# Sinkhorn routing of a fused attention and mixture-of-experts kernel: sums as addition trees and scalings on POOL, reciprocals on DVE

## The chip, the cores and the metric

The kernel runs on one core of one Trainium2 chip. The metric is the device time of one execution in microseconds (us). The engines named below are PE (matrix multiplier), ACT, DVE and POOL (elementwise engines), and SP, whose queue issues nearly all DMA transfers. Each engine takes its own instructions strictly in the order in which the program put them; an instruction whose operand is not ready holds up everything behind it on that engine.

## What is computed

The reference has two parts. The first is chunked attention (4 x 8 heads, 768 positions, head size 64), which produces `x` with N = 3072 tokens of D = 512. The second, which holds most of the work, is a mixture of E = 8 experts whose weights per token come from a Sinkhorn normalisation:

```python
logits = x @ w_gate                      # 3072 x 8
P = np.exp(logits - logits.max())
for _ in range(8):
    P /= P.sum(1, keepdims=True) + 1e-09     # over the 8 experts of a token
    P /= P.sum(0, keepdims=True) + 1e-09     # over the 3072 tokens
    P *= N / E
for e in range(E):
    h = np.maximum(x @ w1[e], 0.0)           # 512 -> 1024
    out += P[:, e:e + 1] * (h @ w2[e])       # 1024 -> 512
```

## The kernel before

The tokens are cut into 6 units of 512. The program works through 48 pairs of expert and unit: all six units for expert 0, then all six for expert 1, and so on. While expert 0 runs, the attention for later units is mixed in between. A product is made in fp16 with each operand split into a high and a low part, by a Strassen-like scheme of seven block products; on PE a block product is six matmuls of 256 columns (line 1593, targets `px`, `py`, `pz` for the hidden layer and `yx`, `yy`, `yz` for the output). Expert 0's output uses plain matmuls of 512 columns instead (line 2121, target `yp`).

The other engines serve PE: DVE and ACT take finished sums out of PSUM (`c<-px`, line 1662, with `q` as the part that ACT read earlier), apply the relu and split the result into high and low parts (`h<-c,h`, line 1720). For the next expert, `cut` (line 601) forms four sums of weight blocks in a buffer `ws` on POOL, and `split` (lines 513 and 521) turns the raw weights `w1f`, `w2f` and the sums `ws` into fp16 pairs `w`, first on ACT, then on DVE. There is one `ws` buffer, so that the next four POOL sums wait until DVE has split the last ones. The same `split` makes the inputs `x<-xt` and `x<-xs`.

The order on every engine is written at build time by a planner (`Plan.run`): each task has an engine, a cost in us, dependencies and a priority (a smaller number goes first), and the planner simulates the engines with these costs and emits instructions in the order in which it starts the tasks. At run time only that order and the semaphores remain.

The routing is one chain of tasks inside this plan. It starts when the logits of all 3072 tokens stand in the tile `lg` (128 partitions x 24 token tiles x 8 experts) and ends with `pscale`, by which expert 0's stored outputs are scaled when expert 1's output first adds to them. One of its eight rounds is: row sums, reciprocal, scaling and column sums per partition (`rows`, all on DVE), a matmul with a matrix of ones that adds the column sums over the 128 partitions (`cp`, line 1529, on PE), and reciprocal and scaling (`columns`, on DVE). PE's instruction stream holds the eight `cp` products between block products of expert 0.

Of the kernel before, what the change touches and what calls it, by code (L numbers as in the profile page):

```python
# [12 lines left out]
F32 = mybir.dt.float32  # L13
I32 = mybir.dt.int32
AF = mybir.ActivationFunctionType
ALU = mybir.AluOpType
AX = mybir.AxisListType
# [73 lines left out]
class Plan:  # L91
# [14 lines left out]
    def add(self, eng, cost, fn, deps=(), prio=0.0, bufs=(), takes=None, frees=None, dma=0.0, many=False):  # L106
        t = Task()
        t.eng, t.cost, t.fn, t.prio, t.takes, t.frees = eng, cost, fn, prio, takes, frees
        t.ready, t.end, t.then, t.n, t.dma = 0.0, None, [], len(self.tasks), dma
        t.many = many  # L110
        if dma:
            t.cost = cost * ISSUE
        before = {id(d): d for d in deps if d is not None}
        for b in bufs:
            assert not b.closed
            before.update({id(d): d for d in b.before})
            b.users.append(t)
        t.left = len(before)
        for d in before.values():
            d.then.append(t)  # L120
        if frees is not None:
            frees.left += 1
        self.tasks.append(t)
        return t
# [109 lines left out]
def tile_chunked_attn_sinkhorn_moe(  # L234
# [27 lines left out]
    nc = tc.nc  # L262
    P = 128
    B, H, S, D = q.shape
    NM = mem_k.shape[2]
    N, DM = out.shape
    E, _, F = w1.shape
# [15 lines left out]
    NT = N // P  # L283
# [7 lines left out]

    misc = ctx.enter_context(tc.tile_pool(name="misc", bufs=1))
    small = ctx.enter_context(tc.tile_pool(name="small", bufs=1))
    xpool = ctx.enter_context(tc.tile_pool(name="xpool", bufs=1))
    wl1 = ctx.enter_context(tc.tile_pool(name="wl1", bufs=1))
    wl2 = ctx.enter_context(tc.tile_pool(name="wl2", bufs=1))
# [13 lines left out]
    late = {}  # L310
# [5 lines left out]
    one = misc.tile([P, 1], F32, name="one")  # L316
    nc.vector.memset(one, 1.0)
    ones = one.broadcast_to([P, P])
# [4 lines left out]
    lg = misc.tile([P, NT, E], F32, name="lg")  # L323
# [15 lines left out]
    add = plan.add  # L339
# [14 lines left out]
    def begin(n):  # L354

        m = min(n, NU - 1)
        return START + m * TURN + (n - m) * UNIT
# [57 lines left out]
    def bank(group, shape, name):  # L415
        return Bank(group, lambda b: banks(b).tile(shape, F32, tag=f"b{b}", name=name))
# [5 lines left out]
    opened = [None]  # L422
# [65 lines left out]
    def turned_max(m, a, t, pool, prio, name):  # L488

        row = bank(pool, [1, P], f"row_{name}")  # L490
        t = add(
            "PE",
            0.35,
            lambda: nc.tensor.transpose(row.t, m, ident),
            [t],
            prio - FIRM,
            takes=row,
        )
        return add(
            "DVE",  # L500
            0.3,
            lambda: nc.vector.tensor_reduce(a, row.t, axis=AX.X, op=ALU.max),
            [t],
            prio,
            frees=row,
        )
# [486 lines left out]
    tr = {}  # L993
# [438 lines left out]
    def attention():  # L1432
# [22 lines left out]
                yield  # L1455
        values(*pend.pop(0))

    def routing(deps):

        box = {}  # L1460

        m, a = most_of[:, 0, -1:], most_of[0:1, 1, -1:]
        urgent = begin(LATE) + 58.5
        t = add(
            "DVE",
            0.35,
            lambda: nc.vector.tensor_reduce(m, lg, axis=AX.XY, op=ALU.max),
            deps,
            urgent,
        )  # L1470
        t = turned_max(m, a, t, "main", urgent, "lg")
        spread = bank("main", [P, 1], "sp_lg")
        t = add(
            "PE",
            0.2,
            lambda: nc.tensor.matmul(spread.t, ones[0:1], a, start=True, stop=True),
            [t],
            urgent - FIRM,
            takes=spread,
        )  # L1480
        t = add("DVE", 0.15, lambda: nc.vector.tensor_copy(m, spread.t), [t], urgent, frees=spread)
        t = add(
            "DVE",
            0.35,
            lambda: nc.vector.tensor_scalar(lg, lg, m, None, op0=ALU.subtract),
            [t],
            urgent,
        )
        t = add("ACT", 0.35, lambda: nc.scalar.activation(lg, lg, AF.Exp), [t], urgent)

        def rows(it):
            def go():
                rs = small.tile([P, NT], F32, tag="rs", bufs=1, name=f"rs_{it}")
                nc.vector.tensor_reduce(rs, lg, axis=AX.X, op=ALU.add)
                nc.vector.tensor_scalar_add(rs, rs, 1e-9)
                nc.vector.reciprocal(rs, rs)
                nc.vector.tensor_tensor(
                    lg, lg, rs[:, :, None].broadcast_to([P, NT, E]), op=ALU.mult
                )
                box[it] = small.tile([P, E], F32, tag="cs", bufs=1, name=f"cs_{it}")  # L1500
                nc.vector.tensor_reduce(
                    box[it], lg.rearrange("p t e -> p e t"), axis=AX.X, op=ALU.add
                )

            return go

        def columns(it, cp):
            def go():
                cr = small.tile([P, E], F32, tag="cr", bufs=1, name=f"cr_{it}")
                nc.vector.tensor_scalar_add(cr, cp.t, 1e-9)  # L1510
                nc.vector.reciprocal(cr, cr)
                nc.vector.scalar_tensor_tensor(
                    lg,
                    lg,
                    float(N) / float(E),
                    cr[:, None, :].broadcast_to([P, NT, E]),
                    op0=ALU.mult,
                    op1=ALU.mult,
                )

            return go

        for it in range(8):
            t = add("DVE", 1.8, rows(it), [t], urgent)
            cp = bank("main", [P, E], f"cp_{it}")
            t = add(
                "PE",
                0.4,
                lambda it=it, cp=cp: nc.tensor.matmul(
                    cp.t, ones, box[it], start=True, stop=True  # L1530
                ),
                [t],
                urgent,
                takes=cp,
            )
            t = add("DVE", 0.8, columns(it, cp), [t], urgent, frees=cp)

        def finish():
            for u in range(NU):
                us = slice(u * TU, (u + 1) * TU)  # L1540
                nc.vector.tensor_scalar(
                    lg[:, us], lg[:, us], ux[:, u : u + 1], 2.0**HSHIFT, op0=ALU.mult, op1=ALU.mult
                )

        return add("DVE", 1.4, finish, [t], urgent)
# [642 lines left out]
    for n, (e, u) in enumerate(units):  # L2188
# [23 lines left out]
        if n == LATE:  # L2212
            while len(lgs) < NU:
                next(feed, None)

            def turn():
                plan.fill = None
                astack.close()
                late["w1"] = ctx.enter_context(tc.tile_pool(name="wr1", bufs=1, side="right"))
                late["w2"] = ctx.enter_context(tc.tile_pool(name="wr2", bufs=1, side="right"))  # L2220
                late["h"] = ctx.enter_context(tc.tile_pool(name="hr", bufs=1, side="right"))
                late["c"] = ctx.enter_context(tc.tile_pool(name="cr", bufs=1, side="right"))
                late["ss"] = ctx.enter_context(tc.tile_pool(name="sr", bufs=1, side="right"))
                for group in ("att", "two"):
                    for b in plan.free[group]:
                        heappush(plan.free["main"], b)
                    plan.free[group] = []

            att_tasks = lgs + [xkept[v] for v in range(KEEP)] + list(gkept.values())
            opened[0] = add("-", 0.0, turn, att_tasks, -2000.0)  # L2230
            for kind, slot in (("w1", 4), ("w2", 4), ("w2", 5), ("h", 4), ("h", 5), ("c", 2), ("ss", 2)):
                rings[kind].after(slot, [opened[0]])
            for kind in ("c", "ss"):
                ring_ = rings[kind]
                ring_.order = [ring_.n % 2, (ring_.n + 1) % 2, 2]
                ring_.n = 0
            for kind, m in (("w1", 5), ("w2", 6), ("h", 6)):
                rings[kind].order = list(range(m))
            rings["w1"].n, rings["w2"].n, rings["h"].n = 4, 4, 4
            routed[0] = routing(lgs)  # L2240
            expert_scale(0, begin(n))
# [81 lines left out]
```

## Time and profile before

| what | value |
|---|---|
| median of 3 runs (lowest to highest) | 1913.08 us (1911.89 to 1914.97) |
| the profiled execution: time / span | 1913.3 us / 1911.5 us |
| granted PE clock | 0.999 |
| PE busy (share of the span) | 1898.8 us (99%) |
| DVE busy | 1468.1 us (77%) |
| ACT busy | 1022.5 us (53%) |
| POOL busy | 503.0 us (26%) |
| first and last of the eight row sums start | 299.8 us, 330.8 us |

The span runs from the first to the last recorded instruction; the time has 1.8 us around it. A busy PE is no proof of PE at its full pace, since a matmul's recorded duration covers its way through the array while the next is already running: the distance between starts shows the pace. Groups of instructions give a count, the total busy time, the mean of one, and after the bar the idle time of the engine before them with what ended it.

### The profile page before, as it was taken

How to read it: one execution, taken by the hardware profiler on the slowest of the kernel's cores; microseconds unless marked ns; L12 is line 12 of the kernel's file. 1: busy time of each engine (PE TensorE's matmuls, PEld its weight loads, DVE VectorE, ACT ScalarE, POOL GpSimd, SP SyncE). 2: the span in 40 equal slices, each digit the busy share in tenths (PEclk: the TensorE clock that was granted, in tenths of full speed). 3: DMA queues.
4: the chain of work that ended last, by engine and by line, in shares of the span. 5: the costliest groups of instructions: out<-in, count | busy, mean ns of one | idle time of the engine just before them, and what ended most of it. 6: DMA issues, size and time to landing. Idle time of an engine off the chain costs nothing.

```text
span 1911.5 us, 47024 instructions
## 1 busy us (share of the span) xinstructions
PE 1898.8 (99%) x19535; PEld 1634.8 (86%) x19535; DVE 1468.1 (77%) x2456; ACT 1022.5 (53%) x1999; POOL 503.0 (26%) x541
## 2 busy tenths in 40 slices
PE   8999999999999999999999999999999999999999
PEld 7777676788888888888888888888888888888888
DVE  5887679878589867898668875898678885786565
ACT  4665555556465545546446544655555563564453
POOL 1210012514134211522224231342124232332112
PEclk9999999999999999999999999999999999999999
DMA  8787653543324432264224433245313632222321
GB/s 198 189 219 182 160 173 133 169 169 106 126 80 160 150 134 77 90 217 165 84 91 154 165 119 114 84 155 188 127 45 111 247 112 97 98 84 83 127 84 67
DMA packets 212998, 254.81 MB, mean 133 GB/s; under 512 B 112240, under 2 KB 146480, under 8 KB 208432
## 3 DMA queue, kind: packets, MB, share of 16 engines
q1 hardware_dynamic: 210660, 251.21, 40.4%
q8 instruction: 153, 2.51, 0.6%
q10 hardware_dynamic: 2124, 0.59, 0.2%
q14 instruction: 61, 0.50, 0.1%
HBM read 187.84 MB, written 63.44 MB: 131 GB/s over the span
## 4 chain that ended last, share of the span: by engine, by line
PE 97%; DVE 2%; SPq 0%; ACT 0%; issue 0%; DMA 0%; POOL 0%; DVEq 0%; POOLq 0%
PE px L1593 26%; PE yx L1593 23%; PE pz L1593 13%; PE yz L1593 11%; PE py L1593 6%; PE yp L2121 6%; PE yy L1593 6%; PE pp L2040 1%; PE xp L1138 1%; PE sp L1071 1%; PE warm L427 1%; DVE w L521 1%; PE ta L1128 1%; PE tk L1012 1%; PE tq L1008 1%; SPq L923 0%
## 5 line engine op out<-in xcount | busy, mean ns | idle before, releaser
L1593 PEld LDWEIGHTS <-w 128*128 128x128 f16 x7896 | 771.2, 98 | 94.4 <-issue 2.8
L1593 PEld LDWEIGHTS <-h 128*128 128x128 f16 x7056 | 690.4, 98 | 81.1 <-issue 0.9
L1593 PE MATMUL px<-x,w 128*128 128x256 f16 x4512 | 547.8, 273 | 1.5 <-DVE c L1662 1.0
L1926 POOL TENSOR_TENSOR acc<-acc,y 128x256 f32<-128x256 f32 x252 | 262.4, 1049 | 881.1 <-ACT y L1901 868.5
L1593 PE MATMUL yx<-w,h 128*128 128x256 f16 x4032 | 467.9, 273 | 0.5 <-DVE acc L1936 0.5
L1652 ACT ACTIVATE q<-px 128x256 f32<-128x256 f32 x376 | 143.1, 382 | 289.6 <-PE px L1593 285.1
L1593 PE MATMUL pz<-x,w 128*128 128x256 f16 x2256 | 278.1, 273 | 0.0
L1593 PE MATMUL yz<-w,h 128*128 128x256 f16 x2016 | 233.8, 273 | 0.0
L1821 DVE TENSOR_TENSOR h<-ss,h 128x1024 f16<-128x1024 f32 x168 | 217.6, 1298 | 3.3 <-ACT h L1797 3.3
L1772 ACT ACTIVATE h<-c 128x768 f16<-128x768 f32 x168 | 140.7, 838 | 112.2 <-DVE c L1662 112.2
L1797 ACT CAST h<-ss 128x1024 f16<-128x1024 f32 x168 | 174.2, 1040 | 39.5 <-DVE ss L1761 39.5
L1761 DVE SCALAR_TENSOR_TENSOR ss<-c,ss 128x256 f32<-128x256 f32 x336 | 176.6, 525 | 8.6
L1805 DVE SCALAR_TENSOR_TENSOR h<-c,h 128x768 f16<-128x768 f32 x168 | 168.7, 1007 | 9.2 <-ACT h L1772 9.1
L1662 DVE SCALAR_TENSOR_TENSOR c<-px,q 128x256 f32<-128x256 f32 x188 | 77.8, 421 | 94.8 <-PE px L1593 85.6
L1901 ACT ACTIVATE y<-yx,pscale 128x256 f32<-128x256 f32 x168 | 79.6, 474 | 120.5 <-PE yx L1593 116.5
L1593 PE MATMUL py<-x,w 128*128 128x256 f16 x1128 | 139.0, 273 | 0.0
L2121 PE MATMUL yp<-w,h 128*128 128x512 f16 x576 | 132.0, 379 | 0.9 <-DVE h L2082 0.9
L1761 DVE SCALAR_TENSOR_TENSOR ss<-c,h 128x512 f32<-128x512 f32 x168 | 125.6, 748 | 1.9 <-ACT h L1749 1.9
L1662 DVE SCALAR_TENSOR_TENSOR c<-py,q 128x256 f32<-128x256 f32 x188 | 78.5, 421 | 62.0 <-PE py L1593 58.7
L1593 PE MATMUL yy<-w,h 128*128 128x256 f16 x1008 | 116.9, 273 | 0.0
L2121 PEld LDWEIGHTS <-h 128*128 128x128 f16 x576 | 55.3, 99 | 60.0 <-DVE h L2082 1.4
L513 ACT ACTIVATE w<-ws,sw 128x1024 f16<-128x1024 f32 (+1 forms) x64 | 69.5, 1090 | 65.7 <-POOL ws L601 65.6
(155 smaller groups left out, 1739.6 us busy)
## 6 DMA issues: line engine op xcount, KB each, us to landing
x<-xkeep SPq DMA_DIRECT2D x28, 1792.0 KB
akeep<-acc SPq DMA_DIRECT2D x168, 256.0 KB
acc<-akeep SPq DMA_DIRECT2D x168, 256.0 KB
w1f<-in_moe_w_dram SPq DMA_DIRECT2D x36, 512.0 KB
w2f<-in_moe_w_dram SPq DMA_DIRECT2D x32, 512.0 KB
w1fm<-in_moe_w_dram SPq DMA_DIRECT2D x28, 512.0 KB
w2fm<-in_moe_w_dram SPq DMA_DIRECT2D x28, 512.0 KB
xkeep<-x SPq DMA_DIRECT2D x6, 1792.0 KB
```

The source lines that it names most:

```text
L513: lambda: nc.scalar.activation(dst(0), src(), AF.Copy, scale=s),
L1593: nc.tensor.matmul(dst.t, a, b, start=(not more and n == 0), stop=(n == end), skip_group_check=more,)
L1652: lambda: nc.scalar.activation(t.t, src.t, AF.Copy, scale=DOWN),
L1662: lambda: nc.vector.scalar_tensor_tensor(c.t[:, o], src.t, DOWN, q.t, op0=ALU.mult, op1=ALU.add),
L1761: lambda: nc.vector.scalar_tensor_tensor(dst(), src(), 0.0, other(), op0=ALU.max, op1=op),
L1772: lambda: nc.scalar.activation(h.t[:, 0, 0:3], c.t, AF.Relu),
L1797: lambda: nc.scalar.copy(h.t[:, 0, 3:7], ss.t),
L1805: lambda: nc.vector.scalar_tensor_tensor(h.t[:, 1, 0:3].rearrange("p a n -> p (a n)"), c.t.rearrange("p a n -> p (a n)"), 0.0, h.t[:, 0, 0 ...
L1821: lambda: spare.tensor_tensor(h.t[:, 1, 3:7], ss.t, h.t[:, 0, 3:7], op=ALU.subtract),
L1901: (lambda: nc.scalar.activation(t.t, src.t, AF.Copy, scale=f))
L1926: lambda: nc.gpsimd.tensor_tensor(acc.t[:, cols], acc.t[:, cols], q.t, op=ALU.add),
L2121: nc.tensor.matmul(py.t, hf.t[:, hl, where[fh], o : o + P], room(fp, WIDE * wl + DM * fh, WIDE * wl + DM * (fh + 1)), start=(fp == 0 and i ...
```

## The change

In each of the eight rounds the row sums become three POOL additions (96, 48 and 24 columns), the row scaling one POOL multiplication of 192 columns, the column sums five POOL additions (96, 48, 24, 8 and 8 columns), and the column scaling one POOL multiplication of 192 columns. DVE keeps the two reciprocals with the additions of 1e-9, and one more instruction on 8 columns that multiplies by N/E. The matmul with ones reads its column sums from the new tile `tree`. The partial results live in `tree`, `row_parts` and `column_parts`. The planner's costs and priorities of these tasks change too: DVE's and PE's parts now go 300 ahead of the rest.

```diff
+        def row_sums():
+            two = tree[0][:, 0 : NT * E // 2].rearrange("p (t e) -> p t e", t=NT)
+            one = tree[0][:, NT * E // 2 :].rearrange("p (t e) -> p t e", t=NT)
+            plus(two, lg[:, :, 0 : E // 2], lg[:, :, E // 2 :])
+            plus(one, two[:, :, 0:2], two[:, :, 2:4])
+            plus(rs, one[:, :, 0], one[:, :, 1])
+        def row_parts():
+            nc.vector.tensor_scalar_add(rr, rs, 1e-9)
+            nc.vector.reciprocal(rr, rr)
+        def over_rows():
+            nc.gpsimd.tensor_tensor(
+                lg, lg, rr[:, :, None].broadcast_to([P, NT, E]), op=ALU.mult
+            )
+            a = tree[0][:, 0 : NT * E // 2].rearrange("p (t e) -> p t e", e=E)
+            b = tree[0][:, NT * E // 2 :].rearrange("p (t e) -> p t e", e=E)
+            plus(a, lg[:, 0 : NT // 2], lg[:, NT // 2 :])
+            plus(b, a[:, 0:6], a[:, 6:12])
+            plus(a[:, 0:3], b[:, 0:3], b[:, 3:6])
+            plus(a[:, 3], a[:, 0], a[:, 1])
+            plus(a[:, 4], a[:, 3], a[:, 2])
+        def column_parts(cp):
+            def go():
+                c = cols_at
+                nc.vector.tensor_scalar_add(c, cp.t, 1e-9)
+                nc.vector.reciprocal(c, c)
+                nc.vector.tensor_scalar_mul(c, c, float(N) / float(E))
+            return go
+        def over_columns():
+            nc.gpsimd.tensor_tensor(
+                lg, lg, cols_at[:, None, :].broadcast_to([P, NT, E]), op=ALU.mult
+            )
         for it in range(8):
-            t = add("DVE", 1.8, rows(it), [t], urgent)
+            t = add("POOL", 1.0, row_sums, [t, opened[0]], urgent)
+            t = add("DVE", 0.5, row_parts, [t], urgent - 300.0)
+            t = add("POOL", 2.1, over_rows, [t], urgent)
             cp = bank("main", [P, E], f"cp_{it}")
...
-                0.4,
+                0.2,
...
-            t = add("DVE", 0.8, columns(it, cp), [t], urgent, frees=cp)
+            t = add("DVE", 0.5, column_parts(cp), [t], urgent - 300.0, frees=cp)
+            t = add("POOL", 0.8, over_columns, [t], urgent)
```

The removed functions `rows` and `columns` stand in the listing above; `plus(to, a, b)` is one POOL addition.

What the change makes of the order is shown at three places. The first is DVE, in the round that belongs to the third `cp` product (rounds are counted from 0, and the round called 2 here is the one that ends with this product). Names: `c<-px`, `c<-pz` are the PSUM reads for unit 5, `w_1_..` weights of expert 1, `h_5_..` hidden layers of unit 5. Before, the stretch from one column reciprocal to the next reads:

```order
L1510 TENSOR_SCALAR cr_5530<-cp_5508 128x8
L1511 RECIPROCAL cr_5530<-cr_5530 128x8
L1512 SCALAR_TENSOR_TENSOR lg<-lg,cr_5530 128x192
L1494 TENSOR_REDUCE rs_5551<-lg 128x24
L1495 TENSOR_SCALAR rs_5551<-rs_5551 128x24
L1496 RECIPROCAL rs_5551<-rs_5551 128x24
L1497 TENSOR_TENSOR lg<-lg,rs_5551 128x192
L1501 TENSOR_REDUCE cs_5556<-lg 128x8
L1662 SCALAR_TENSOR_TENSOR c_5_0_5505<-px_5_0_5449,q_0_5_0_5541 128x256
L1662 SCALAR_TENSOR_TENSOR c_5_1_5526<-px_5_1_5461,q_0_5_1_5564 128x256
L1662 SCALAR_TENSOR_TENSOR c_5_0_5505<-pz_5_0_5517,q_0_5_0_5524 128x256
L1662 SCALAR_TENSOR_TENSOR c_5_1_5526<-pz_5_1_5534,q_0_5_1_5528 128x256
```

After, behind the reciprocals of the second `cp` product:

```order
L522 SCALAR_TENSOR_TENSOR w_1_1_5528<-w2f_1_5417,sw,w_1_1_5528 128x512
L1683 SCALAR_TENSOR_TENSOR c_5_0_5520<-px_5_0_5468,q_0_5_0_5554 128x256
L522 SCALAR_TENSOR_TENSOR w_1_1_5528<-w2f_1_5417,sw,w_1_1_5528 128x256
L1683 SCALAR_TENSOR_TENSOR c_5_1_5530<-px_5_1_5476,q_0_5_1_5568 128x256
L1508 TENSOR_SCALAR row_parts<-row_parts 128x24
L1509 RECIPROCAL row_parts<-row_parts 128x24
L1683 SCALAR_TENSOR_TENSOR c_5_0_5520<-pz_5_0_5534,q_0_5_0_5541 128x256
L1683 SCALAR_TENSOR_TENSOR c_5_1_5530<-pz_5_1_5547,q_0_5_1_5543 128x256
L522 SCALAR_TENSOR_TENSOR w_1_0_5436<-ws_1_0_5438,sw,w_1_0_5436 128x1024
L1741 SCALAR_TENSOR_TENSOR h_5_0_5622<-c_5_0_5520,h_5_0_5622 128x1024
L1741 SCALAR_TENSOR_TENSOR h_5_1_5639<-c_5_1_5530,h_5_1_5639 128x1024
L1526 TENSOR_SCALAR column_parts<-cp_5645 128x8
```

The eight routing instructions that stood in a row have become two short groups, and splits of expert 1's weights, which came later before, stand between them.

The second place is POOL over the same round, from the column scaling that opens it. Before, POOL had nothing but the sums `ws` of expert 1 in this part of the program:

```order
L601 TENSOR_TENSOR ws_1_0_5422<-w1f_0_5341 128x256
L601 TENSOR_TENSOR ws_1_0_5422<-ws_1_0_5422,w1f_0_5341 128x256
L601 TENSOR_TENSOR ws_1_0_5422<-w1f_0_5341 128x256
L601 TENSOR_TENSOR ws_1_0_5422<-w1f_0_5341,ws_1_0_5422 128x256
L601 TENSOR_TENSOR ws_1_0_5766<-w2f_0_5469 128x256
```

After:

```order
L602 TENSOR_TENSOR ws_1_0_5438<-w1f_0_5350 128x256
L602 TENSOR_TENSOR ws_1_0_5438<-w1f_0_5350,ws_1_0_5438 128x256
L1533 TENSOR_TENSOR lg<-lg,column_parts 128x192
L1498 TENSOR_TENSOR tree<-lg 128x96
L1498 TENSOR_TENSOR tree<-tree 128x48
L1498 TENSOR_TENSOR row_parts<-tree 128x24
L1512 TENSOR_TENSOR lg<-lg,row_parts 128x192
L1498 TENSOR_TENSOR tree<-lg 128x96
L1498 TENSOR_TENSOR tree<-tree 128x48
L1498 TENSOR_TENSOR tree<-tree 128x24
L1498 TENSOR_TENSOR tree<-tree 128x8 x2
L602 TENSOR_TENSOR ws_1_0_5641<-w2f_0_5443 128x256
```

Ten routing instructions per round now share POOL's queue with the `ws` sums, of which up to three in a row stand between them.

The third place is PE around the third `cp` product. Before, it stood ahead of unit 5's last `px` block product:

```order
L1593 MATMUL pz_5_1_5534<-x_5278,w_0_1_664 128x256
L1529 MATMUL cp_5581<-cs_5556,one 128x8
L1593 LDWEIGHTS w_0_0_658
L1593 MATMUL px_5_0_5449<-x_5278,w_0_0_658 128x256
L1593 LDWEIGHTS w_0_0_658
```

After, it stands 24 matmuls further on, in the middle of a plain output `yp` of unit 4:

```order
L2142 MATMUL yp_5624<-w_0_1_1172,h_4_1_5253 128x512
L1545 MATMUL cp_5645<-tree,one 128x8
L2142 LDWEIGHTS h_4_2_5466
L2142 MATMUL yp_5624<-w_0_2_359,h_4_2_5466 128x512
L2142 LDWEIGHTS h_4_2_5466
```

Apart from the places of the eight `cp` products PE's order is the same instruction for instruction. Between the products stood 42, 42, 24, 24, 18, 18 and 18 other matmuls before; now 60, 54, 36, 30, 48, 60 and 66. No DMA is added or removed; on SP the loads of `w1f` and `w2f` for expert 1 and the stores of `yp` results (`akeep<-acc`) change places within a stretch of eleven.

More of the change, by code (lines that the diff above doesn't have):

```diff
@@ L293, in tile_chunked_attn_sinkhorn_moe @@
     small = ctx.enter_context(tc.tile_pool(name="small", bufs=1))
+    tree = []
     xpool = ctx.enter_context(tc.tile_pool(name="xpool", bufs=1))
@@ L1456, in attention @@
         values(*pend.pop(0))
+    halves_at = small.tile([P, 2, NT], F32, name="row_parts")
+    cols_at = small.tile([P, E], F32, name="column_parts")
     def routing(deps):
@@ L1489, in routing @@
         t = add("ACT", 0.35, lambda: nc.scalar.activation(lg, lg, AF.Exp), [t], urgent)
-        def rows(it):
-            def go():
[L1493 to L1503, printed above, removed]
-            return go
@@ L1507, in columns @@
[L1507 to L1521, printed above, removed]
+        rs, rr = halves_at[:, 0], halves_at[:, 1]
@@ new lines, in plus @@
+        def plus(to, a, b):
+            nc.gpsimd.tensor_tensor(to, a, b, op=ALU.add)
+        def row_sums():
[7 more added lines that the diff above has]
+            nc.vector.reciprocal(rr, rr)
@@ L1527, in routing @@
                 "PE",
-                0.4,
-                lambda it=it, cp=cp: nc.tensor.matmul(
-                    cp.t, ones, box[it], start=True, stop=True
+                0.2,
+                lambda cp=cp: nc.tensor.matmul(
+                    cp.t,
+                    ones,
+                    tree[0][:, 4 * E : 5 * E],
+                    start=True,
+                    stop=True,
                 ),
                 [t],
-                urgent,
+                urgent - 300.0,
                 takes=cp,
             )
-            t = add("DVE", 0.8, columns(it, cp), [t], urgent, frees=cp)
+            t = add("DVE", 0.5, column_parts(cp), [t], urgent - 300.0, frees=cp)
+            t = add("POOL", 0.8, over_columns, [t], urgent)
         def finish():
@@ L2223, in turn @@
                 late["ss"] = ctx.enter_context(tc.tile_pool(name="sr", bufs=1, side="right"))
+                late["t"] = ctx.enter_context(tc.tile_pool(name="tr", bufs=1, side="right"))
+                tree.append(late["t"].tile([P, NT * E // 2 + NT * E // 4], F32, name="tree"))
                 for group in ("att", "two"):
```

## The prediction

> **What bounds the kernel now.** I read the page first: its busy table, then the chain that ended last.
>
> ```profile
> PE 1898.8 (99%) x19535; PEld 1634.8 (86%) x19535; DVE 1468.1 (77%) x2456; ACT 1022.5 (53%) x1999; POOL 503.0 (26%) x541
> PE 97%; DVE 2%; SPq 0%; ACT 0%; issue 0%; DMA 0%; POOL 0%; DVEq 0%; POOLq 0%
> ```
>
> PE sets the end. Of its 12.7 us of idle time (1911.5 - 1898.8) the view by stretches tells where it lies, and how busy the others are around the routing:
>
> ```profile
> 0.00:100.00 100.00, 93.45 (x1636) 71.04 (x1636) 73.54 (x135) 55.49 (x110) 21.01 (x29) 0.98 0.78 191
> 300.00:320.00 20.00, 20.00 (x158) 15.18 (x157) 18.53 (x52) 13.34 (x26) 2.83 (x4) 1.00 0.49 171
> 320.00:340.00 20.00, 20.00 (x124) 12.07 (x123) 18.85 (x50) 5.84 (x11) 5.13 (x7) 1.00 0.32 106
> 1500.00:1912.00 412.00, 408.39 (x3741) 365.74 (x3738) 287.74 (x476) 198.83 (x390) 97.12 (x99) 1.00 0.29 101
> ```
>
> The columns after the bounds are PE, PEld, DVE, ACT and POOL. 6.6 us of idle lie in the first 100 us and 3.6 in the last 412, both far from the routing, which runs at 300 to 335. There DVE is busy 18.5 to 18.9 of 20 us, POOL 3 to 5, and PE all 20. Since PE's records overlap, its pace has to be read from its timeline:
>
> ```profile
> 302.33 0.29 PE L1529 MATMUL cp<-cs,one 128*128 128x8 f32 x2
> 302.47 2.78 PE L1593 MATMUL px<-x,w 128*128 128x256 f16 x24
> 305.09 1.47 PE L1593 MATMUL py<-x,w 128*128 128x256 f16 x12
> 315.81 0.28 PE L1529 MATMUL cp<-cs,one 128*128 128x8 f32 x2
> 315.95 5.34 PE L2121 MATMUL yp<-w,h 128*128 128x512 f16 x24
> 321.13 0.28 PE L1529 MATMUL cp<-cs,one 128*128 128x8 f32 x2
> 325.15 0.28 PE L1529 MATMUL cp<-cs,one 128*128 128x8 f32 x2
> ```
>
> From start to start, 24 matmuls of 256 columns take 2.62 us (0.109 each), 24 of 512 columns 5.18 us (0.216 each), a `cp` product 0.14 us. Groups follow each other at this pace through the routing: PE waits for nothing, the eight `cp` products included. So a relief of DVE has nothing to shorten here, while anything that comes late for PE is paid in full.
>
> **What is removed.** The groups of DVE in 300 to 400 us:
>
> ```profile
> L1501 DVE TENSOR_REDUCE cs<-lg 128x8 f32<-128x192 f32 x8 | 4.0, 501 | 0.3
> L1512 DVE SCALAR_TENSOR_TENSOR lg<-lg,cr 128x192 f32<-128x192 f32 x8 | 3.2, 404 | 0.3
> L1497 DVE TENSOR_TENSOR lg<-lg,rs 128x192 f32<-128x192 f32 x8 | 3.1, 394 | 0.3
> L1494 DVE TENSOR_REDUCE rs<-lg 128x24 f32<-128x192 f32 x8 | 2.8, 352 | 0.2
> L1496 DVE RECIPROCAL rs<-rs 128x24 f32<-128x24 f32 x8 | 2.4, 303 | 0.3
> L1511 DVE RECIPROCAL cr<-cr 128x8 f32<-128x8 f32 x8 | 1.6, 203 | 0.3
> L1495 DVE TENSOR_SCALAR rs<-rs 128x24 f32<-128x24 f32 x8 | 1.5, 181 | 0.3
> L1510 DVE TENSOR_SCALAR cr<-cp 128x8 f32<-128x8 f32 x8 | 1.3, 159 | 0.2 <-PE cp L1529 0.2
> ```
>
> The first four go: 4.0 + 3.2 + 3.1 + 2.8 = 13.1 us of DVE. Eight multiplications on 8 columns come, like the 159 ns row: 1.3 us. DVE gains 11.8 us, all beside PE's work: worth 0. PE's own work is the same 16 matmuls: 0.
>
> **What is added on POOL.** Its rows: fixed cost, one operand, and four additions of 128x256 without DVE in the way (columns: start, duration).
>
> ```profile
> L2309 POOL MEMSET const-float32-1.0<- 128x1 f32 x1 | 0.1, 99 | 0.0
> L915 POOL COPY w<-v_pair 128x1040 f32<-128x1040 f32 x2 | 2.1, 1052 | 11.0 <-DMA v_pair<-in_v_dram 11.0
> 329.85 0.73 POOL L601 TENSOR_TENSOR ws<-w2f 128x256 f32<-128x256 f32 x1 [26.68 <-DVE cr L1510]
> 330.66 0.73 POOL L601 TENSOR_TENSOR ws<-ws,w2f 128x256 f32<-128x256 f32 x1
> ```
>
> No POOL addition as short as the new ones is in this trace, so I bound it. With the memset's 0.10 us as the fixed part, a column costs (0.73 - 0.10)/256 = 2.46 ns. With twice the copy's rate per column (2 x 0.91 = 1.82 ns) the fixed part is 0.73 - 0.47 = 0.26 us. A round has 10 instructions and 96+48+24 + 192+96+48+24+8+8 + 192 = 736 columns: 2.81 us by the first, 3.94 by the second; I take the middle, 0.18 us and 2.15 ns, which is 3.38 us, since nothing puts it nearer to either. Between dependent POOL instructions lie 330.66 - 330.58 = 0.08 us, 8 times a round: 0.64. Over eight rounds POOL gets 27 us more, of which it has room.
>
> **The new chain of one round.** It is serial over four engines, and its end is an instruction of PE. From `cp` to DVE:
>
> ```profile
> 325.47 0.17 DVE L1510 TENSOR_SCALAR cr<-cp 128x8 f32<-128x8 f32 x1 [0.25 <-PE cp L1529]
> ```
>
> That is 0.32 us after the `cp` at 325.15. The column part is 0.16 + 0.20 + 0.16 = 0.52, the row part 0.18 + 0.30 = 0.48. The four other handovers (DVE to POOL twice, POOL to DVE, POOL to PE) I put at 0.13 each, an estimate between POOL's 0.08 and the 0.18 that is left of 0.32 after `cp`'s own 0.14: 0.52. Sum: 0.32 + 0.52 + 0.48 + 0.52 + 0.64 + 3.38 = **5.86 us** without disturbance (5.3 to 6.4 with POOL's ends).
>
> **What PE allows for it.** The order moves the `cp` products apart; at PE's pace the 60, 54 (42 of 256 and 12 of 512 columns), 36 and 30 (all 512), 48 (30 and 18), 60 and 66 matmuls between them last, with one `cp`, 6.68, 7.30, 7.90, 6.60, 7.29, 6.68 and 7.33 us. Undisturbed, the chain fits into all seven.
>
> **What disturbs it.** DVE instructions with two operands in SBUF and POOL's additions hold each other up. Two pairs show it:
>
> ```profile
> 344.85 1.35 DVE L1720 SCALAR_TENSOR_TENSOR h<-c,h 128x1024 f16<-128x1024 f32 x1 [0.54 <-ACT h L1711]
> 345.19 1.59 POOL L601 TENSOR_TENSOR ws<-ws,w2f 128x256 f32<-128x256 f32 x1
> 347.03 1.52 DVE L1720 SCALAR_TENSOR_TENSOR h<-c,h 128x1024 f16<-128x1024 f32 x1
> 347.43 1.71 POOL L601 TENSOR_TENSOR ws<-w2f,ws 128x256 f32<-128x256 f32 x1
> ```
>
> The same POOL addition takes 0.86 and 0.98 us longer than 0.73 and ends about one free addition after DVE's end. Undisturbed lengths of such DVE work, from start to start:
>
> ```profile
> 319.72 1.21 DVE L1720 SCALAR_TENSOR_TENSOR h<-c,h 128x1024 f16<-128x1024 f32 x1
> 320.86 0.74 DVE L521 SCALAR_TENSOR_TENSOR w<-w1f,sw,w 128x512 f16<-128x512 f32 x1
> 321.52 0.16 DVE L1510 TENSOR_SCALAR cr<-cp 128x8 f32<-128x8 f32 x1
> 328.05 0.47 DVE L521 SCALAR_TENSOR_TENSOR w<-w1f,sw,w 128x256 f16<-128x256 f32 x1
> 328.44 1.28 DVE L521 SCALAR_TENSOR_TENSOR w<-ws,sw,w 128x1024 f16<-128x1024 f32 x1
> ```
>
> 1.14 us for 1024 columns, 0.66 for 512, 0.39 for 256. In the new order the rounds hold: round 1 two of 1024, one of 512, one of 256 (3.33 us); round 2 three, one and one (4.47); round 3 one, three and three (4.29); round 4 none; rounds 5 and 6 one of 1024 each (1.14); round 7 as round 1 (3.33). Each either stands ahead of a chain step in DVE's queue or meets a POOL addition. Of a length of 1.14 the two POOL rows lost 0.75 and 0.86; since some will meet nothing I charge 0.75 of all. Excess over PE's time: round 1: 5.86 + 2.50 - 6.68 = 1.68; round 2: 5.86 + 3.35 - 7.30 = 1.91; round 3: 5.86 + 3.22 - 7.90 = 1.18. Rounds 4 to 7: -0.74, -0.57, +0.04, +1.03, which cancel. So 4.77 us.
>
> The Trainium skill (SBUF — State Buffer, "Who interferes with whom") says that a DVE instruction with two SBUF inputs and a GpSimd instruction that reads SBUF exclude each other, the second waiting until the first is over. Charged in full on every instruction, rounds 1 to 3 would give 2.51 + 3.03 + 2.25 = 7.79 in place of 4.77; the trace agrees with the waiting itself (0.86 and 0.98 us), not with a collision every time.
>
> The first `cp`, six matmuls earlier than before, is due at 302.33 - 6 x 0.109 = 301.68. On DVE the first row part follows the split `x<-xt`, after which the trace has
>
> ```profile
> 298.24 0.42 DVE L1662 SCALAR_TENSOR_TENSOR c<-py,q 128x256 f32<-128x256 f32 x1
> ```
>
> so it starts there: 298.24 + 0.48 + 0.13 + POOL's six instructions (6 x 0.18 + 376 x 0.00215 + 5 x 0.08 = 2.29) + 0.13 = 301.27. In its way are one split of 1024 and one of 256: 0.75 x 1.53 = 1.15, so 302.42: PE waits 0.74.
>
> **Sum:** 4.77 + 0.74 = 5.5 us later, against the profiled execution's own 1913.3 us (which stands 0.2 above the median 1913.08; span 1911.5 and 1.8 around it): **1918.8 us**. PE's idle time away from both ends of the span is 12.7 - 6.6 - 3.6 = 2.5 us, so later work can't make this up.
>
> **Costed at nothing.** (a) PSUM reads `c<-px`, `c<-pz` stand behind DVE's new waits for POOL; PE's next product on such a sum comes 12 matmuls (1.31 us) later, and where it waits, it waits together with the `cp` ahead; without that cover a round pays its rest once more. (b) `ws` sums wait among the routing's POOL work, and the splits after them; but the order puts the `w<-ws` that expert 1's first unit needs ahead of unit 5's last PSUM reads, where it was behind them. If it is late, PE stops at the first block that needs a weight sum. (c) On SP, loads for expert 1 go ahead of stores of `yp` results, and wait for their stage buffer there; four result buffers cover a store's delay. (d) `pscale` comes over 20 us later; it is first used by expert 1's outputs, a unit and more behind.
>
> **Rivals.** Hidden anyway: the collisions fall into gaps and PE hardly waits. For it: 5.86 is below every distance. Against it: rounds 1 to 3 hold 12 us of DVE work in the way. With a charge c rounds 0 to 3 cost 13.62c - 4.71, so at half they cost 2.1 us (1915.4) and the change passes 0.2% (3.8 us, about what a measurement of this kernel can tell from no change) at c = 0.625. Chance 0.28.
>
> Full collisions: every one is paid in full, by the mechanism of the two pairs. Rounds 1 to 3 give 7.79, rounds 4 to 7 together 1.15, the first `cp` 1.12: 10.1 us, 1923.4; with POOL's high cost (chain 6.42) it is 14.3 us, 1927.6. Against: the first of the pairs lost 0.75. Chance 0.14. This is what the page cited above would make of it.
>
> Faster: DVE, at 18.5 to 18.9 of 20 us the next bound, loses 11.8 us, and PE gains where it waited for PSUM reads. It decides from the point where PE has such waits; idle away from both ends is 2.5 us, so at best 1910.8, and the pace rows show none in the routing. Chance 0.03 for over 0.2%, which it could only reach through waits hidden in PE's records.
>
> The forecast with a partial charge (0.625 to 0.9): chance 0.55. So slower 0.55 + 0.14 = 0.69, same 0.28, faster 0.03. The range runs from 1913.8 (nearly all hidden) to 1925 (full charge with a POOL cost above the middle); what it leaves out is the 0.03, the lowest few hundredths of the hidden case and the dearest part of the full one.
>
> **What would show it.** PE's timeline should have gaps ahead of the first four `cp` products, about 0.7, 1.7, 1.9 and 1.2 us, the idle put down to POOL `tree`, none at the fifth to seventh, and a last pace unchanged. A POOL round should take near 4 us free (short additions of 0.18 to 0.35 us), with additions stretched where DVE splits run. DVE should be some 12 us less busy with new waits for POOL. I am wrong if the short additions cost over 0.4 us (then all rounds are late and the time passes 1925), if they slip between DVE's instructions without loss (then 1913 to 1915), or if PE stops elsewhere, at a weight sum or a PSUM bank.

## The result and the profile after

The changed kernel takes 1923.43 us (median of 6 runs, 1920.39 to 1923.74). Its ratio to the kernel before is 1.0053, 95% interval 1.0040 to 1.0066: slower by 8 to 13 us, inside the predicted range and above the predicted 1918.8. The profiled execution took 1923.57 us with a span of 1921.7. One of the six executions of the kernel before in this comparison took 2449.49 us and stays out of the ratio; the other five took 1911.23 to 1914.97.

The page's busy table and the head of its chain, as before:

```profile
PE 1900.6 (99%) x19535; PEld 1634.3 (85%) x19535; DVE 1460.0 (76%) x2432; ACT 1022.5 (53%) x1999; POOL 540.3 (28%) x621
PE 94%; DVE 2%; POOL 2%; issue 1%; DMA 1%; ACT 1%; SPq 0%; ACTq 0%; DVEq 0%; POOLq 0%
```

POOL has come into the chain that sets the end. By stretches (columns after the bounds: PE, PEld, DVE, ACT, POOL) PE is no longer busy all the time around the routing, DVE has become much idler there, and POOL is busy for 78 and 84% of it:

```profile
300.00:320.00 20.00, 18.18 (x156) 14.98 (x155) 16.18 (x34) 12.68 (x25) 15.57 (x27) 1.00 0.63 224
320.00:340.00 20.00, 17.13 (x83) 7.86 (x82) 11.38 (x22) 6.94 (x12) 16.88 (x33) 1.00 0.19 66
```

The table of PE's waits names the place (total, number of times, longest):

```profile
PE cp L1545 <- POOL tree L1498: 6.3, 6, 1.7
```

PE's timeline has all eight `cp` products, here with the block products around the second:

```profile
304.69 0.39 PE L1545 MATMUL cp<-tree,one 128*128 128x8 f32 x2 [0.33 <-POOL tree L1498]
310.82 0.82 PE L1614 MATMUL pz<-x,w 128*128 128x256 f16 x6
313.14 0.39 PE L1545 MATMUL cp<-tree,one 128*128 128x8 f32 x2 [1.50 <-POOL tree L1498]
313.38 0.81 PE L1614 MATMUL pz<-x,w 128*128 128x256 f16 x6
322.38 0.39 PE L1545 MATMUL cp<-tree,one 128*128 128x8 f32 x2 [1.67 <-POOL tree L1498]
331.76 0.39 PE L1545 MATMUL cp<-tree,one 128*128 128x8 f32 x2 [1.20 <-POOL tree L1498]
338.47 0.28 PE L1545 MATMUL cp<-tree,one 128*128 128x8 f32 x2
345.77 0.29 PE L1545 MATMUL cp<-tree,one 128*128 128x8 f32 x2
353.08 0.39 PE L1545 MATMUL cp<-tree,one 128*128 128x8 f32 x2 [0.46 <-POOL tree L1498]
361.87 0.39 PE L1545 MATMUL cp<-tree,one 128*128 128x8 f32 x2 [1.18 <-POOL tree L1498]
```

The bracketed idle time counts from the modelled end of the matmul before and so shows a little less than the loss. The loss is the displacement of the next product: without a wait the six `pz` matmuls from 310.82 end their turn at 311.47 (6 x 0.109), the `cp` adds 0.14, and the next `pz` would start at 311.61; it starts at 313.38, 1.77 us late. In the same way the eight products cost 0.60, 1.77, 1.94, 1.46, 0, 0, 0.73 and 1.45 us, together **7.95 us**.

### The profile page after: what moved, and what is told of

Same layout as the page of the kernel before. It is cut to its first block, busy times and chain, and to the rows that moved or that the text cites. A ratio compares the mean times of both kernels' runs of the same rounds, so it can differ in the third digit from the quotient of the medians.

```text
span 1921.7 us, 47094 instructions
## 1 busy us (share of the span) xinstructions
PE 1900.6 (99%) x19535; PEld 1634.3 (85%) x19535; DVE 1460.0 (76%) x2432; ACT 1022.5 (53%) x1999; POOL 540.3 (28%) x621
## 3 DMA queue, kind: packets, MB, share of 16 engines
q8 instruction: 153, 2.51, 0.5%
## 4 chain that ended last, share of the span: by engine, by line
PE 94%; DVE 2%; POOL 2%; issue 1%; DMA 1%; ACT 1%; SPq 0%; ACTq 0%; DVEq 0%; POOLq 0%
PE px L1614 25%; PE yx L1614 23%; PE pz L1614 12%; PE yz L1614 11%; PE py L1614 6%; PE yy L1614 6%; PE yp L2142 6%; PE xp L1139 1%; PE pp L2061 1%; POOL tree L1498 1%; PE sp L1072 1%; PE ta L1129 1%; PE tk L1013 1%; PE tq L1009 1%; DMA k<-in_k_dram 0%
```

## The experiments

Theory: the loss is PE waiting for POOL at the `cp` products, because DVE instructions with two SBUF operands and POOL's short additions shut each other out. Rivals: the splits delay the chain by standing ahead of it in DVE's queue, with no collision; POOL's additions are long in themselves; the loss lies partly elsewhere.

**One operand instead of two.** All queues keep their order; only the form of 32 DVE instructions changes.

```diff
+    def single(o, i):
+        with nc.allow_low_precision(reason="a copy"):
+            nc.vector.tensor_reduce(o, i.unsqueeze(len(i.shape)), axis=AX.X, op=ALU.add)
...
-            lambda: nc.vector.scalar_tensor_tensor(
-                dst(1), src(), s, dst(0), op0=ALU.mult, op1=ALU.subtract
+            (
+                (lambda: single(dst(1), src()))
+                if alone
+                else lambda: nc.vector.scalar_tensor_tensor(
+                    dst(1), src(), s, dst(0), op0=ALU.mult, op1=ALU.subtract
+                )
             ),
...
```

`alone` holds for expert 1's weights; the hidden splits of units 4 and 5 are changed in the same way.

> The changed kernel with the same order on every engine, but the DVE halves of expert 1's weight splits and of the hidden splits of units 4 and 5 under expert 0 read one SBUF operand instead of two: a reduction over an axis of length one, equally wide, in the same place of DVE's queue. The kernel leaves out the low halves of these splits (copies stand in their place). Collision theory (DVE instructions with two SBUF operands and POOL's additions shut each other out): POOL's additions keep their free length, the waits at the cp products fall from 8 us to under 1, the time is 1913 to 1916. Queue theory (the splits cost what they cost by standing ahead of the chain in DVE's queue): waits stay near 8 us, 1921 to 1924. Third theory (part of the loss lies outside the routing, the 2.5 us by which the profiled execution was already late before it): 2 to 3 us stay, 1915 to 1916, with no wait at cp.

Measured: 1913.99 us, ratio 1.0002 (0.9992 to 1.0011): the loss is gone, but for 2 us at most that the interval leaves room for. The third `cp` product, with POOL's row scaling and tree ahead of it, beside the same stretch of DVE:

```profile
313.35 1.21 DVE L511 TENSOR_REDUCE w<-ws 128x1024 f16<-128x1024 f32 x1
314.48 2.33 DVE L511 TENSOR_REDUCE h<-c 128x1024 f16<-128x1024 f32 x2
...
312.75 0.52 POOL L1523 TENSOR_TENSOR lg<-lg,row_parts 128x192 f32<-128x192 f32 x1 [0.63 <-DVE row_parts L1520]
313.35 0.39 POOL L1509 TENSOR_TENSOR tree<-lg 128x96 f32<-128x96 f32 x1
313.81 1.17 POOL L1509 TENSOR_TENSOR tree<-tree 128x48 f32<-128x48 f32 x4
...
316.71 0.28 PE L1556 MATMUL cp<-tree,one 128*128 128x8 f32 x2
```

In the changed kernel the same place read:

```profile
317.84 1.28 DVE L522 SCALAR_TENSOR_TENSOR w<-ws,sw,w 128x1024 f16<-128x1024 f32 x1
319.03 2.64 DVE L1741 SCALAR_TENSOR_TENSOR h<-c,h 128x1024 f16<-128x1024 f32 x2
...
317.39 0.52 POOL L1512 TENSOR_TENSOR lg<-lg,row_parts 128x192 f32<-128x192 f32 x1 [0.63 <-DVE row_parts L1509]
317.99 1.37 POOL L1498 TENSOR_TENSOR tree<-lg 128x96 f32<-128x96 f32 x1
319.44 2.89 POOL L1498 TENSOR_TENSOR tree<-tree 128x48 f32<-128x48 f32 x4
```

The 96-column addition takes 1.37 us against 0.39, the four that follow 2.89 against 1.17: 2.7 us in this round, lost to three DVE instructions of 1024 columns. With reductions of the same width in the same place POOL runs at its free lengths. So the queue theory falls. Of the displacements only the first product's is left, 0.59 us; its chain meets the splits `x<-xt`, which still read two operands here (beside them the tree's 96-column addition takes 1.25 us):

```profile
302.60 0.39 PE L1556 MATMUL cp<-tree,one 128*128 128x8 f32 x2 [0.33 <-POOL tree L1509]
```

No loss elsewhere shows, and of the 2 to 3 us of the third theory the interval allows hardly more than the lower end.

**Larger planned costs.** The program computes the same; only the planner's idea of POOL changes.

```diff
-            t = add("POOL", 1.0, row_sums, [t, opened[0]], urgent)
+            t = add("POOL", 1.6, row_sums, [t, opened[0]], urgent)
...
-            t = add("POOL", 2.1, over_rows, [t], urgent)
+            t = add("POOL", 3.6, over_rows, [t], urgent)
...
-            t = add("POOL", 0.8, over_columns, [t], urgent)
+            t = add("POOL", 1.2, over_columns, [t], urgent)
```

> The changed kernel with larger planned costs for the three POOL tasks of a round (1.6, 3.6 and 1.2 in place of 1.0, 2.1 and 0.8), which the planner alone sees: the cp products stand 9.2 to 11.8 us apart on PE instead of 6.6 to 7.9, everything computed stays. Theory that PE's whole loss is waiting for POOL at the cp products: no wait there, 1912.5 to 1915. Rival (DVE's waits for POOL delay PSUM reads, or POOL's work delays expert 1's weights): PE waits at other products, 1916 to 1922. Second rival (a loss outside the routing): 2 to 3 us stay, 1915 to 1916.

Measured: 1913.72 us, ratio 1.0002 (0.9993 to 1.0010). Of the waits at `cp` only 0.22 us at the seventh is left (its next product comes 0.47 us late):

```profile
363.86 0.39 PE L1545 MATMUL cp<-tree,one 128*128 128x8 f32 x2 [0.22 <-POOL tree L1498]
```

The collisions are still there, as a column scaling (0.59 us free) and the last four additions of a tree (1.17 us free) of the second round show:

```profile
303.58 1.50 POOL L1533 TENSOR_TENSOR lg<-lg,column_parts 128x192 f32<-128x192 f32 x1
309.67 2.02 POOL L1498 TENSOR_TENSOR tree<-tree 128x48 f32<-128x48 f32 x4
```

They cost next to nothing, because the `cp` products stand later in PE's order. The loss is thus the meeting of two things: a POOL that is slower than planned, and a PE order that has it wait for POOL. Either one taken away is enough. This version is level with the kernel before, not ahead of it: no gain was found in anything that POOL took off DVE.

**Collisions made on purpose, and their control.** The round that ends with the fifth `cp` has no split and no wait. Two instructions are added behind its row reciprocals, with two operands in one kernel and with one in the other (the output tile is read by nobody).

```diff
             nc.vector.reciprocal(rr, rr)
+            rounds[0] += 1
+            if rounds[0] == 5:
+                wide = ident[:, None, :].broadcast_to([P, 8, P])
+                for _ in range(2):
+                    nc.vector.scalar_tensor_tensor(
+                        tree[1], wide, 0.0, wide, op0=ALU.max, op1=ALU.subtract
+                    )
...
+                tree.append(late["t"].tile([P, 8, P], F16, name="extra"))
```

The other kernel has a `tensor_reduce` of `wide` over an axis of length one in place of the `scalar_tensor_tensor`.

> The changed kernel with two added DVE instructions in the round that ends with the fifth cp product, which had no split and no wait: 1024 columns each, two SBUF operands, written to a tile that nobody reads, right behind the row reciprocals. Collision theory: POOL's six instructions of this round lose about 2.1 us to them (two of 1.07), 0.5 us of which the round had to spare, so PE waits 1.5 to 1.7 us at the fifth cp, where it waited for nothing. Rival (POOL's short instructions slip between DVE's): no wait there.

> The same with two reductions over an axis of length one, which read one SBUF operand and are as wide. Collision theory: no wait at the fifth cp, POOL's six instructions at their free lengths. Rival (any DVE work at that place delays the chain): the same wait as with two operands.

Measured once each: 1926.21 and 1919.93 us. Most of the 6.28 us between them is not the added collision: PE's product `row_lg`, which stands ahead of the routing, starts at 290.39 us in the one and at 286.55 in the other, 3.84 apart, and the first `cp` product adds 0.69 (1.28 us late against 0.59). What the added instructions do is read from the rows of their round. With two operands (DVE, two POOL rows, PE):

```profile
336.61 2.61 DVE L1516 SCALAR_TENSOR_TENSOR extra<-ident 128x1024 f16<-128x1024 f32 x2
...
336.77 1.37 POOL L1521 TENSOR_TENSOR lg<-lg,row_parts 128x192 f32<-128x192 f32 x1 [0.45 <-DVE row_parts L1511]
338.22 1.25 POOL L1498 TENSOR_TENSOR tree<-lg 128x96 f32<-128x96 f32 x1
...
340.76 0.39 PE L1554 MATMUL cp<-tree,one 128*128 128x8 f32 x2 [1.06 <-POOL tree L1498]
```

With one:

```profile
332.10 2.42 DVE L1517 TENSOR_REDUCE extra<-ident 128x1024 f16<-128x1024 f32 x2
...
332.26 0.52 POOL L1522 TENSOR_TENSOR lg<-lg,row_parts 128x192 f32<-128x192 f32 x1 [0.45 <-DVE row_parts L1511]
332.86 0.39 POOL L1498 TENSOR_TENSOR tree<-lg 128x96 f32<-128x96 f32 x1
...
335.02 0.28 PE L1555 MATMUL cp<-tree,one 128*128 128x8 f32 x2
```

Each two-operand instruction costs POOL 0.85 us (1.37 - 0.52, 1.25 - 0.39), 1.71 together and not the 2.1 expected; PE's next product comes 1.33 us late, a little under the expected 1.5 to 1.7. Each one-operand instruction of the same width costs POOL nothing, and PE does not wait. The Trainium skill (SBUF — State Buffer, "Who interferes with whom") states that a DVE instruction with two SBUF inputs contends with a GpSimd instruction that reads SBUF, and that `tensor_reduce` never does. Both parts agree with these rows: 0.85 us lost to each two-operand instruction, nothing to the reductions. Of 1.14 us per DVE instruction POOL paid 0.85; its row scaling starts 0.16 us behind the first of them and can meet only what is left of it.

**Without one DVE addition.** The addition of 1e-9 to the row sums is left out.

```diff
-            nc.vector.tensor_scalar_add(rr, rs, 1e-9)
-            nc.vector.reciprocal(rr, rr)
+            nc.vector.reciprocal(rr, rs)
```

> The changed kernel with the same order, without the addition of 1e-9 to the row sums (left out; DVE takes the reciprocal at once). Theory that DVE's one-operand addition in SBUF is also shut out by the POOL sum ws that the order puts between row sums and row scaling (0.68 us in place of 0.18 in rounds 1, 3, 4, 5 and 7): the chain shortens by 0.2 us in every round and by 0.5 more in those, of which the rounds that end with a wait (0 to 3, 6, 7) show about 2.5 us: 1920.5 to 1921.5. Rival (only the splits matter, the addition hides behind the ws sum, which POOL has to finish anyway): under 1 us, 1922.5 to 1923.5.

Measured: 1921.93 us, ratio 1.0046 (1.0034 to 1.0059), which by time can't be told from the changed kernel. By the profile the displacements at `cp` sum to 6.5 us, 1.45 less: between the two expectations. The changed kernel's second round shows the addition held up beside a `ws` sum, and the same round of this kernel shows what came of removing it:

```profile
307.96 0.73 POOL L602 TENSOR_TENSOR ws<-ws,w1f 128x256 f32<-128x256 f32 x1
...
308.04 0.69 DVE L1508 TENSOR_SCALAR row_parts<-row_parts 128x24 f32<-128x24 f32 x1 [0.47 <-POOL row_parts L1498]
...
309.14 1.37 POOL L1512 TENSOR_TENSOR lg<-lg,row_parts 128x192 f32<-128x192 f32 x1 [0.45 <-DVE row_parts L1509]
```

Without the addition:

```profile
304.22 0.73 POOL L602 TENSOR_TENSOR ws<-ws,w1f 128x256 f32<-128x256 f32 x1
...
304.30 0.30 DVE L1508 RECIPROCAL row_parts<-row_parts 128x24 f32<-128x24 f32 x1 [0.47 <-POOL row_parts L1498]
304.52 1.51 DVE L1740 SCALAR_TENSOR_TENSOR h<-c,h 128x1024 f16<-128x1024 f32 x1
...
304.91 1.50 POOL L1511 TENSOR_TENSOR lg<-lg,row_parts 128x192 f32<-128x192 f32 x1
```

The reciprocal runs beside the `ws` sum at its full speed and, counted from the start of that sum, begins 0.72 us earlier. POOL's row scaling begins only 0.49 us earlier (0.69 us in place of 1.18 behind the start), because POOL has to finish the `ws` sum first; beside the 1024-column split it then takes 1.50 us in place of 1.37. So 0.36 us of 0.72 are left, and the second product's displacement falls by as much, from 1.77 to 1.41 us. At the eighth product nothing is gained (1.49 us against 1.45).

**The sums alone.** Trees on POOL, both scalings on DVE as before the change.

```diff
+            nc.vector.tensor_tensor(
+                lg, lg, rr[:, :, None].broadcast_to([P, NT, E]), op=ALU.mult
+            )
...
-            t = add("POOL", 2.1, over_rows, [t], urgent)
+            t = add("POOL", 1.4, over_rows, [t], urgent)
...
-            t = add("POOL", 0.8, over_columns, [t], urgent)
```

The added multiplication stands in `row_parts`; the column scaling goes back into `column_parts` in the same way, and `over_rows` keeps the five additions alone.

> One part of the change alone: sums as trees on POOL, both scalings back on DVE (as in the kernel before), planned costs fitted to it. Chain of a round without disturbance: 0.32 + 0.72 + 1.05 + 0.84 + 1.61 + 0.4 = 4.9 us against distances between the cp products of 5.3 to 7.9 us. Collision theory: eight short POOL additions instead of ten, and shorter ones, meet the same splits; waits of 2 to 5 us, 1915 to 1918. Rival (POOL's two scalings carry the loss, the trees nothing): no wait, 1912.5 to 1914. Rival (the trees carry all): 1920 to 1923.

Measured: 1919.64 us, ratio 1.0032 (1.0019 to 1.0044), with all eight `cp` products displaced, by 7.05 us in sum: more than the 2 to 5 expected, and nearly the whole change's 7.95. The time lies between the ranges of the collision theory and of the rival in which the trees carry all. The additions alone are thus enough for most of such a loss, in the order that was planned for them. But that order is another: the planner, told of shorter rounds, put the `cp` products as close as 5.3 us, so that less POOL work bought no more room. So this run does not divide the 7.95 us between additions and scalings.

**Once more.** The changed kernel unaltered.

> The changed kernel once more, to see how much of its 10 us are the waits at the cp products. If these waits (8.0 us of displaced products in the profile) are all, the ratio comes to 1.0042 (1921) and the waits appear again at the same six products with about the same lengths. If something beside them is lost in every execution, 1.0055 (1923.5).

Measured: 1920.24 us, ratio 1.0035 (1.0023 to 1.0047). The wait row is the same:

```profile
PE cp L1545 <- POOL tree L1498: 6.2, 6, 1.7
```

This interval and the first one share 1.0040 to 1.0047, 7.7 to 9.0 us, and the 7.95 us of the profile lie there. The profiled execution of the first comparison reached the first `cp` product 2.5 us later than the kernel before (due at 304.19 against 301.68), the one here 0.6 us later. Up to the routing the order is the same on all engines, and the 2.5 us are there before it: PE's product `row_lg` starts at 289.99 us against 287.47. A lower granted clock goes with them. In both executions it was 0.91 from 20 to 40 us, and in the changed kernel's it fell once more, from 60 to 80 us (the third column from the right; kernel before, changed kernel):

```profile
60.00:80.00 20.00, 18.43 (x311) 11.09 (x310) 19.38 (x28) 13.83 (x26) 10.19 (x9) 1.00 0.73 180
60.00:80.00 20.00, 19.29 (x361) 10.92 (x360) 17.69 (x26) 12.65 (x24) 10.42 (x9) 0.92 0.78 185
```

The other late execution, that of the collisions made on purpose (`row_lg` at 290.39 us), has two such stretches as well, at 0.93 and 0.90. With one, `row_lg` stood at 287.5 and 288.0 us (the kernel before, and the changed kernel once more). Without any, it stood at 285.3 to 286.6 us in four executions, but at 287.9 in that with single operands, so that the clock is not all of it, and it was not tested as a cause. No systematic loss beside the waits shows.

## Why the prediction was right, and where it was off

*Direction and place.* PE had no slack in the routing, DVE's relief was worth nothing (both the kernel with other costs and the one with single operands sit at the old time with 8 to 15 us less DVE work), and PE stopped at `cp` for POOL's `tree`. All as forecast, except that the seventh product, for which no gap was forecast, has one, and that DVE became 8.1 us less busy (1468.1 to 1460.0) and not some 12. One reading of the profile before was off without weight for the sum: the last stretch, 1500 to 1912, reaches 0.5 us past the end of the span, so 3.1 and not 3.6 us of PE's idle time lie in it, and 3.0 and not 2.5 away from both ends.

*POOL's price.* The chosen 0.18 us plus 2.15 ns per column held: undisturbed additions of 96, 48, 24 and 8 columns take 0.39, 0.27, 0.23 and 0.20 us, the scalings 0.52 and 0.59. A round's ten add up to 0.39 + 0.27 + 0.23 + 0.52 + 0.39 + 0.27 + 0.23 + 0.20 + 0.20 + 0.59 = 3.29 us against the 3.38 used.

*The charge.* 0.75 of every two-operand instruction gave 0.74, 1.68, 1.91 and 1.18 us at the first four products; measured were 0.60, 1.77, 1.94 and 1.46: 5.77 against 5.5. Made on purpose, a collision cost 0.85 of 1.14, which is 0.75. But that the sum came out is partly luck, as the rounds of the changed kernel show when they are taken apart (us):

| round that ends at | charged | POOL's routing instructions over their free lengths | held up between DVE and POOL |
|---|---|---|---|
| second `cp` | 2.50 | 2.20 | 0.52 |
| third | 3.35 | 3.20 | 0.30 |
| fourth | 3.22 | 2.16 | 1.47 |
| seventh | 0.86 | 0.86 | 0.83 |
| eighth | 2.50 | 2.35 | 0.70 |

The last column is what the two ways over DVE take beyond 0.69 us (from the start of the column addition to the column scaling) and 0.62 us (from the end of the row sums to the row scaling), their lengths in rounds where no `ws` sum is in the way. What is left of a round without both columns is 5.7 us, against the 5.86 of the prediction. So in the first three of these rounds the collisions took at most 7.56 of 12.09 us, 0.63 and not 0.75, and a term that the prediction does not have, 2.29 us there, made up for much of it.

*The step that failed:* "Rounds 4 to 7: -0.74, -0.57, +0.04, +1.03, which cancel." They do not. The next round's chain starts from the `cp` product itself, and PE issues that at its place in the order, however early `tree` is ready. Time to spare in a round is lost with it, so only positive terms may be added: by the prediction's own numbers 5.5 + 0.04 + 1.03 = 6.6 us, 1919.9. The profile shows 0, 0, 0.73 and 1.45 at these four. In the round that ends at the fifth product, for one, the tree was ready at 337.95 us (336.78 + 1.17), PE started the product at 338.47, and the next round began no earlier for it. What remains in the last two (2.18 against 1.07) is mostly the term that was left out, the last column of the table: POOL's `ws` sums stand between the routing's steps. The prediction had them wait for the routing, under "Costed at nothing" (b), but not the routing for them. DVE's additions and multiplications with one operand take longer beside such a sum, and POOL's next routing instruction waits until the sum is done. In the seventh round the multiplication by N/E took 0.47 us in place of 0.17 and the addition of 1e-9 0.37 in place of 0.18; besides, that addition stood behind a PSUM read `c<-px` for which DVE waited for PE. In the eighth the addition took 0.68 us, but two `ws` sums held the row scaling up anyway:

```profile
357.63 0.73 POOL L602 TENSOR_TENSOR ws<-ws,w1f 128x256 f32<-128x256 f32 x1
358.31 0.73 POOL L602 TENSOR_TENSOR ws<-w1f 128x256 f32<-128x256 f32 x1
359.00 0.97 POOL L1512 TENSOR_TENSOR lg<-lg,row_parts 128x192 f32<-128x192 f32 x1
...
357.71 0.68 DVE L1508 TENSOR_SCALAR row_parts<-row_parts 128x24 f32<-128x24 f32 x1 [0.47 <-POOL row_parts L1498]
```

That fits the kernel without the addition, which gained 0.37 us at the seventh product and nothing at the eighth. By itself this term does not make PE wait: with single operands the addition still took 0.69 us in the round of the second product, and PE waited there for nothing. With 7.95 us in place of 5.5 the forecast would have been 1921.3.

*The rivals.* "Hidden anyway" was the smaller chance and did not happen, though it takes only other planner costs to make it happen. "Full collisions" named 1923.4, nearest to the first median, but it has too much at the first `cp` products (2.51, 3.03, 2.25 at the second to fourth against 1.77, 1.94, 1.46); the nearness is an accident of the offset before the routing. At the last two products its terms, 0.32 and 1.86, add up to the measured 2.18, but the split is another (0.73 and 1.45), and POOL lost less there than it charges. Of what was costed at nothing, the loads, the weight sums and `pscale` showed no wait of PE of their own.

## What to carry to other kernels

When the bounding engine has no idle time where a change sits, a relief of another engine is worth nothing, and only what can make the bounding engine wait counts: write down the new chain from one fixed instruction of that engine to the next, and compare it with the time between them. Add only the rounds that come late, since an early result does not bring forward an instruction that has its place in an in-order queue. A schedule written from free durations is wrong where two engines shut each other out; here raising the costs of the slowed engine repaired it, and the tree sums on POOL then cost nothing, but won nothing either.

## What the runs showed of the hardware

- A one-operand DVE addition on 24 fp32 columns, SBUF to SBUF, is held up by POOL's sum (0.68 us in place of 0.17), while a reciprocal on the same operand at the same place is not (0.30 us beside a running sum), and 1024-column reductions leave POOL's additions at their free lengths.
- Very short POOL additions are nearly all fixed cost: 8 columns 0.20 us, 24 columns 0.23 us, 256 columns 0.73 us.
